# First layers of a mixture block queued behind given attention matmuls on TensorE, in a fused attention and MLP kernel

## The chip, the cores and the metric

One core of one Trainium2 chip runs the whole kernel. The metric is the device time of one execution in microseconds, lower is better; the median of several runs is compared. The engines are TensorE (PE, its weight loads PEld), VectorE (DVE), ScalarE (ACT), GpSimd (POOL) and SyncE (SP), which issues the DMAs. Each works through its own queue in the order that the built program gives.

## The reference, cut to what matters

```python
# q, k, v: (8 batches, 8 heads, 576 tokens, 64); w_phi: (64, 128); all float32
def phi(x):
    proj = einsum('bhsd,df->bhsf', x, w_phi)
    proj = proj - max(abs(proj), axis=-1, keepdims=True)
    return concatenate([exp(proj), exp(-proj)], axis=-1)      # 256 features
q_p, k_p = phi(q), phi(k)
kv = einsum('bhsf,bhsd->bhfd', k_p, v)
z = sum(k_p, axis=2)
x = einsum('bhsf,bhfd->bhsd', q_p, kv) / (einsum('bhsf,bhf->bhs', q_p, z)[..., None] + 1e-6)
x = x.transpose(0, 2, 1, 3).reshape(4608, 512)                # tokens by model
h = x @ w_in                                                  # 512 -> 2048
out = maximum(0.01 * h, h) @ w_out                            # 2048 -> 512
```

## The kernel before

**Two parts beside each other.** The attention makes `x`, two heads at a time: head pair i = 4 * batch + pair, 32 of them. The MLP works on blocks of 256 tokens, 18 of them, and needs all four pairs of the batches that a block touches. Block 2 (tokens 512 to 767) and block 3 need batch 1 (pairs 4 to 7); block 4 (tokens 1024 to 1279) also needs batch 2 (pairs 8 to 11), since batch 2 begins at token 1152.

**Precision.** A factor is split into a high part in the fast float32r format and a low part that holds the rest (`xh` and `xl`, `gh` and `gl`, `qh` and `ql`, `kph` and `kpl`, weights `w0h`, `w0l`, `w1h`, `w1l`), and a product is three matmuls: high by high, high by low, low by high.

**A unit of the MLP** is one block and one of 16 slices of 128 hidden features. `layer1` has 12 matmuls of 256 columns into the PSUM tile `h` (2 buffers): L601 and L602 read `xh`, L604 reads `xl`, each for d = 0 to 3, and the head pairs of a batch are the four d. ScalarE then applies the leaky ReLU in place (Prelu, L607) and casts `gh` (L69), VectorE makes `gl` (L609). `layer2` has six matmuls of 512 columns into two `acc` tiles (L623, L624, L625). It is written three units later (LAG = 3). The list `steps` gives the units their numbers from 0: 0 to 7 are the first half of block 0, 8 to 23 block 1, 24 to 31 the rest of block 0, 32 to 47 block 2, 48 to 63 block 3, 64 to 79 block 4. `split(i)` casts a block's `x` from `ring` into `xh` (ScalarE, L69) and `xl` (GpSimd, L74); there is one buffer of each.

**The attention** is the generator `attention()`, which takes turns between `k_phase` of one pair and `q_phase` (or `token_q_phase` for the first 8 pairs) of the pair ahead of it. For the pairs around unit 60: `q_phase` has projections (L377, L378), a transpose and a maximum on VectorE (L379, L381, small reductions at L383 to L389), the subtraction and transpose back into `mb` (L398, L400, one buffer), exponentials on ScalarE (L405, L406), the cast `qh` (L69), `ql` on GpSimd (L74), six matmuls per half and head (L417, L418, L420), and copies to `ring` and `tq` (L422, L423). At the end VectorE and GpSimd divide by the denominators (L426 to L431), so that `ring` holds `x`. `k_phase` has projections (L302 or L231), maximum, subtraction, exponentials `ek` (L249, L250), the casts `kph` and `kpl`, and sums into the PSUM tile `c` (L211); then transposes (L281).

**What sets the order.** The program is written unit by unit; `advance(goal)` between them draws from the generator. Attention is traced at a priority (PA = -500000) ahead of the MLP's (0). A scheduler then puts each engine's queue in an order by these priorities and by its own estimate of when an instruction could start. So where attention and MLP instructions stand to each other in a queue is not written in the code, but comes out of that estimate. On the chip the engines take their queues in that order.

Of the kernel before, what the change touches and what calls it, by code (L numbers as in the profile page):

```python
# [28 lines left out]
NBLK = NTOK // T  # L29
LAG = 3  # L30
CUT = 8
NN = 8
NK = 8
NF = 12
# [12 lines left out]
def attention_moe_kernel(ctx: ExitStack, tc: tile.TileContext, q, k, v, vt, w_phi, w_in, w_out, out):  # L47
    nc = tc.nc
# [7 lines left out]
    def st(shape, dt, tag):  # L56
        return sp.tile(shape, dt, tag=tag, name=tag, bufs=BUFS.get(tag, 1))
# [8 lines left out]
    def copy_(key, o, i):  # L66
        e = pick(key) or "a"
        if e == "a":
            nc.scalar.copy(o, i)  # L69
        else:  # L70
            (nc.vector if e == "v" else nc.gpsimd).tensor_copy(o, i)
# [4 lines left out]
    def pt(tag):  # L76
        return ps.tile([P, 512], F32, tag=tag, name=tag, bufs=PBUFS[tag])
# [5 lines left out]
    def weight(which, part, ft):  # L83
        g, f = divmod(ft, 4)
        if (which, part, g) not in weights:
            name = f"w{which}{part}{g}"
            weights[which, part, g] = (cp.tile([P, 4, DM], F32R, tag="late", name=name, bufs=4) if g == 3 else
                                       ct([P, 4, DM], F32R, name))
        return weights[which, part, g][:, f]
# [101 lines left out]
    def k_phase(i):  # L191
# [87 lines left out]
        for j in range(2):  # L279
            for t in range(2):  # L280
                nc.tensor.transpose(kvtv[:, j, t], kvs[:, j, t], ident[0:66, 0:66])  # L281
        if i < NN:
            kvh = st([P, 2, 2, P], F32, "kvx" if i % 2 else "kvh")
# [286 lines left out]
    def attention():  # L570
        for i in range(NP, B * NP + 1):
            gens = [k_phase(i)] if i < B * NP else []
            if i > NP:
                gens.append((token_q_phase if i - 1 < NN else q_phase)(i - 1))
            while gens:
                for it in list(gens):
                    if next(it, end) is end:
                        gens.remove(it)
                    else:
                        yield i - 1  # L580
            yield i
# [4 lines left out]
    def split(i):  # L586
        for d in range(NP):
            t0 = 0
            while t0 < T:
                c = (i * T + t0) % (2 * S)  # L590
                n = min(T - t0, S - c % S)
                x = ring[:, c // S, d, c % S : c % S + n]
                t1 = t0 + n
                copy_("xh", xh[:, d, t0:t1], x)
                tt_("xl", xl[:, d, t0:t1], x, xh[:, d, t0:t1].bitcast(F32), ALU.subtract)
                t0 = t1

    def layer1(i, ft):
        ph = pt("h")[:, 0:T]
        for d in range(NP):  # L600
            nc.tensor.matmul(ph, lhsT=weight(0, "h", ft)[:, d * P : d * P + P], rhs=xh[:, d], start=d == 0, stop=False)  # L601
            nc.tensor.matmul(ph, lhsT=weight(0, "l", ft)[:, d * P : d * P + P], rhs=xh[:, d], start=False, stop=False)  # L602
        for d in range(NP):
            nc.tensor.matmul(ph, lhsT=weight(0, "h", ft)[:, d * P : d * P + P], rhs=xl[:, d], start=False, stop=d == NP - 1)  # L604
        gh = st([P, T], F32R, "gh")
        gl = st([P, T], F32R, "gl")
        nc.scalar.activation(ph, ph, AF.Prelu, alpha=0.01)  # L607
        copy_("gh", gh, ph)
        nc.vector.tensor_tensor(gl, ph, gh.bitcast(F32), op=ALU.subtract)  # L609
        gs[i, ft] = (gh, gl)  # L610
# [3 lines left out]
    def layer2(i, ft, half=range(TT)):  # L614
        first, last = (ft in (0, CUT), ft in (CUT - 1, NFT - 1)) if i == 0 else (ft == 0, ft == NFT - 1)
        if first and half[0] == 0:
            for t in range(TT):
                accs[i, t] = pt("acc")
        gh, gl = gs[i, ft]
        for t in half:  # L620
            ts = slice(t * P, t * P + P)
            a = accs[i, t]
            nc.tensor.matmul(a, lhsT=gh[:, ts], rhs=weight(1, "h", ft), start=first, stop=False)  # L623
            nc.tensor.matmul(a, lhsT=gh[:, ts], rhs=weight(1, "l", ft), start=False, stop=False)  # L624
            nc.tensor.matmul(a, lhsT=gl[:, ts], rhs=weight(1, "h", ft), start=False, stop=last)  # L625
        if not last:
            return
        for t in half:
            if ft == CUT - 1:
                if t == 0:  # L630
                    held[0] = st([P, TT, DM], F32, "ks")
                copy_("o", held[0][:, t], accs[i, t])
                continue
            o = st([P, DM], F32, "ek" if i == NBLK - 1 and t else "o")
            if i == 0:
                nc.vector.tensor_tensor(o, accs[i, t], held[0][:, t], op=ALU.add)
            else:
                copy_("o", o, accs[i, t])
            r = i * T + t * P
            nc.sync.dma_start(out[r : r + P, :], o)  # L640

    stream = attention()
    state = {"p": PA, "n": NP - 1}

    def advance(goal):
        keep = tc.cur_priority
        tc.cur_priority = state["p"]
        while state["n"] < goal:
            state["n"] = max(state["n"], next(stream, B * NP))
        state["p"] = tc.cur_priority  # L650
        tc.cur_priority = keep

    def room(i):
        return min(B, 2 + i * T // S) * NP
# [15 lines left out]
    steps = [(i, ft) for i in range(2, NBLK) for ft in range(NFT)]  # L670
    steps = [(0, ft) for ft in range(CUT)] + [(1, ft) for ft in range(NFT)] + [(0, ft) for ft in range(CUT, NFT)] + steps
    split(0)
    for n, (i, ft) in enumerate(steps):
        layer1(i, ft)
        advance(min(room(n // NFT + 1), NP * (1 + (n + 1) / NFT * T / S) + 2))
        if n + 1 < len(steps) and steps[n + 1][0] != i:
            advance(math.ceil((steps[n + 1][0] + 1) * T / S) * NP)
            split(steps[n + 1][0])
        if n >= LAG:
            layer2(*steps[n - LAG])  # L680
# [39 lines left out]
```

## Time and profile before

| | us |
|---|---|
| median of 3 runs | 1193.41 (1190.35 to 1195.17) |
| the profiled execution's own time | 1196.45 |
| its span, first to last instruction | 1194.7 |
| TensorE busy | 1164.5 (97%) |
| ScalarE busy | 833.5 (70%) |
| VectorE busy | 755.9 (63%) |
| GpSimd busy | 417.5 (35%) |

The profile's rows name an operation by the line of the source, the engine and the tiles, out<-in. A wait is shown as the idle time of the engine ahead of an instruction and what ended it. Busy time of TensorE holds the modelled ends of overlapped matmuls, so that a busy TensorE can still be slower than it could be; the spacing of neighbouring matmuls shows that. In the table of stretches the granted clock is TensorE's, 1.00 at full speed.

### The profile page before, as it was taken

The numbers are of one execution on the slowest core, as the hardware profiler recorded it, in microseconds if no ns is written. First come the engines' busy times: TensorE is split into PE (matmuls) and PEld (weight loads), VectorE is DVE, ScalarE is ACT, GpSimd is POOL, SyncE is SP. The second block draws the span as 40 slices with busy tenths as digits, with TensorE's granted clock in tenths as the row PEclk, the third lists the DMA queues.
The fourth block names the chain that finished last, engine by engine and source line by source line (L and its number), as shares of the span: only waits on it lengthen the run. The fifth ranks groups of instructions, "written<-read, shape, count | busy, mean of one in ns | idle before, by whom it ended". The sixth has DMA issues, their size and how long they took to land.

```text
span 1194.7 us, 21190 instructions
## 1 busy us (share of the span) xinstructions
PE 1164.5 (97%) x7576; PEld 1045.5 (88%) x7576; DVE 755.9 (63%) x1510; ACT 833.5 (70%) x2108; POOL 417.5 (35%) x422
## 2 busy tenths in 40 slices
PE   8899999999998999999999999999999999999998
PEld 5687888899897989889899999998999999988987
DVE  4899883566767777677787777726777776111111
ACT  4898884667777787878788888837787877432232
POOL 0111011345454444545455454604454544110000
PEclk9899999999998999999999999999999999999999
DMA  7334532111201111110111111101011100000000
GB/s 208 90 101 142 152 114 59 40 42 31 60 22 50 32 50 31 41 30 22 50 31 50 32 49 32 49 12 37 23 50 32 49 1 19 1 18 19 1 19 18
DMA packets 62778, 57.01 MB, mean 48 GB/s; under 512 B 45136, under 2 KB 46288, under 8 KB 62672
## 3 DMA queue, kind: packets, MB, share of 16 engines
q1 hardware_dynamic: 62672, 55.65, 16.4%
q8 instruction: 60, 0.98, 0.4%
q14 instruction: 46, 0.38, 0.1%
HBM read 46.20 MB, written 9.44 MB: 47 GB/s over the span
## 4 chain that ended last, share of the span: by engine, by line
PE 82%; DVE 8%; ACT 5%; issue 2%; DMA 1%; POOL 1%; SPq 0%; DVEq 0%; ACTq 0%; POOLq 0%
PE h L601 10%; PE h L604 10%; PE h L602 10%; PE acc L623 10%; PE acc L625 10%; PE acc L624 10%; PE c L211 7%; PE a L302 2%; PE a L420 2%; PE a L418 2%; PE a L417 2%; PE a L231 2%; PE a L333 1%; PE a L377 1%; PE a L378 1%
## 5 line engine op out<-in xcount | busy, mean ns | idle before, releaser
L601 PE MATMUL h<-xh,w0h 128*128 128x256 f32 x1152 | 296.3, 287 | 5.9 <-DVE gl L609 4.9
L602 PE MATMUL h<-xh,w0l 128*128 128x256 f32 x1152 | 290.9, 282 | 0.0
L609 DVE TENSOR_TENSOR gl<-h,gh 128x256 fp32r<-128x256 f32 x288 | 118.7, 416 | 245.9 <-ACT gh L69 220.6
L623 PE MATMUL acc<-w1h,gh 128*128 128x512 f32 x576 | 229.6, 399 | 6.4 <-ACT gh L69 6.3
L601 PEld LDWEIGHTS h<-xh,w0h 128*128 128x128 f32 x1152 | 218.0, 189 | 17.0 <-DVE gl L609 8.0
L624 PE MATMUL acc<-w1l,gh 128*128 128x512 f32 x576 | 227.7, 395 | 0.0
L602 PEld LDWEIGHTS h<-xh,w0l 128*128 128x128 f32 x1152 | 217.9, 189 | 7.0 <-issue 0.4
L607 ACT ACTIVATE h<-h 128x256 f32<-128x256 f32 x288 | 105.3, 368 | 155.0 <-PE h L604 152.0
L625 PE MATMUL acc<-w1h,gl 128*128 128x512 f32 x576 | 204.4, 396 | 0.0
L604 PE MATMUL h<-xl,w0h 128*128 128x256 f32 x1152 | 200.3, 283 | 0.0
L74 POOL TENSOR_TENSOR ql<-eq,qh 128x576 fp32r<-128x576 f32 x96 | 146.5, 1539 | 73.6 <-ACT qh L69 51.0
L604 PEld LDWEIGHTS h<-xl,w0h 128*128 128x128 f32 x1152 | 164.5, 189 | 1.1 <-issue 0.4
L74 POOL TENSOR_TENSOR kpl<-ek,kph 128x512 fp32r<-128x512 f32 x72 | 96.6, 1342 | 146.9 <-PE c L211 67.2
L623 PEld LDWEIGHTS acc<-w1h,gh 128*128 128x128 f32 x576 | 108.4, 188 | 27.7 <-ACT gh L69 8.9
L624 PEld LDWEIGHTS acc<-w1l,gh 128*128 128x128 f32 x576 | 108.4, 188 | 18.0
L69 ACT CAST gh<-h 128x256 fp32r<-128x256 f32 x288 | 105.1, 371 | 25.6 <-PE acc L624 20.0
L74 POOL TENSOR_TENSOR xl<-ring,xh 128x256 fp32r<-128x256 f32 (+3 forms) x100 | 62.6, 655 | 162.1 <-PE h L604 131.6
L74 POOL TENSOR_TENSOR ring<-ring,mb 128x576 f32<-128x576 f32 (+2 forms) x45 | 49.8, 1108 | 192.9 <-DVE mb L559 39.2
L625 PEld LDWEIGHTS acc<-w1h,gl 128*128 128x128 f32 x576 | 99.3, 189 | 8.1
L249 ACT ACTIVATE ek<-pmk 128x256 f32<-128x256 f32 (+1 forms) x128 | 53.3, 417 | 33.5 <-POOL kpl L74 17.3
L199 DVE TENSOR_TENSOR ks<-rk,ks 64x576 fp32r<-64x576 f32 x40 | 44.5, 1112 | 30.5 <-ACT ks L69 29.9
L211 PE MATMUL c<-kph,vh 128*66 128x256 f32 x240 | 62.1, 281 | 0.7 <-ACT kph L69 0.7
(214 smaller groups left out, 2257.8 us busy)
## 6 DMA issues: line engine op xcount, KB each, us to landing
out_dram<-o SPq DMA_DIRECT2D x35, 256.0 KB, 2.1
rk<-in_k_dram SPq DMA_DIRECT2D x29, 288.0 KB, 2.8
ring<-in_w_in_dram SPq DMA_DIRECT2D x16, 512.0 KB, 3.6
qh<-in_w_out_dram SPq DMA_DIRECT2D x16, 512.0 KB, 3.7
rq<-in_q_dram SPq DMA_DIRECT2D x28, 288.0 KB, 3.0
rv<-in_v_dram SPq DMA_DIRECT2D x29, 256.0 KB, 3.5
rv<-in_vt_dram SPq DMA_DIRECT2D x58, 32.0 KB, 3.0
fr<-in_k_dram SPq DMA_DIRECT2D x2, 288.0 KB, 3.4
```

The costliest lines, as they stand in the source:

```text
L69: nc.scalar.copy(o, i)
L74: (nc.vector if pick(key) == "v" else nc.gpsimd).tensor_tensor(o, a, b, op=op)
L211: nc.tensor.matmul(kvp[0 : lt.shape[1], 256 * j : 256 * j + 256], lhsT=lt, rhs=rt, start=first and j == 0, stop=last, skip_group_check=True)
L249: nc.scalar.activation(ek[r, :, 0:F], pmk[r, 2 * s : 2 * s + 2], AF.Exp)
L601: nc.tensor.matmul(ph, lhsT=weight(0, "h", ft)[:, d * P : d * P + P], rhs=xh[:, d], start=d == 0, stop=False)
L602: nc.tensor.matmul(ph, lhsT=weight(0, "l", ft)[:, d * P : d * P + P], rhs=xh[:, d], start=False, stop=False)
L604: nc.tensor.matmul(ph, lhsT=weight(0, "h", ft)[:, d * P : d * P + P], rhs=xl[:, d], start=False, stop=d == NP - 1)
L607: nc.scalar.activation(ph, ph, AF.Prelu, alpha=0.01)
L609: nc.vector.tensor_tensor(gl, ph, gh.bitcast(F32), op=ALU.subtract)
L623: nc.tensor.matmul(a, lhsT=gh[:, ts], rhs=weight(1, "h", ft), start=first, stop=False)
L624: nc.tensor.matmul(a, lhsT=gh[:, ts], rhs=weight(1, "l", ft), start=False, stop=False)
L625: nc.tensor.matmul(a, lhsT=gl[:, ts], rhs=weight(1, "h", ft), start=False, stop=last)
```

## The change

While attention is traced, the TensorE instructions that it makes are collected in `products`, numbered from 0 in the order of the program. The first layers of units 24 to 61 are traced inside `tc.issue_after(...)`, which gives each of their TensorE instructions an edge to one product: unit n may stand in TensorE's queue only behind product 111 + 10.2 * (n - 24), rounded down. An edge within one engine's queue needs no semaphore; it is an order and no wait of its own. Unit 24's product is 111, unit 57's 447, unit 58's 457 and unit 61's 488. The rest of the program is as it was, but the scheduler works all queues out anew with these edges.

```diff
+PACED = (24, 62, 111, 10.2)
+PE = mybir.EngineType.PE
...
+    products = []
     stream = attention()
     state = {"p": PA, "n": NP - 1}
...
         while state["n"] < goal:
+            made = len(nc.cur_bb.bb.instructions)
             state["n"] = max(state["n"], next(stream, B * NP))
+            products.extend(i for i in nc.cur_bb.bb.instructions[made:] if i.engine == PE)
...
     for n, (i, ft) in enumerate(steps):
-        layer1(i, ft)
+        if PACED[0] <= n < PACED[1]:
+            with tc.issue_after(products[int(PACED[2] + PACED[3] * (n - PACED[0]))]):
+                layer1(i, ft)
+        else:
+            layer1(i, ft)
```

The lines of the changed kernel stand two further down than before in the attention and in both layers (L601 is L603, L417 is L419, L69 is L71).

What it moves, first on TensorE at unit 57, whose `h` is `h_4004` and whose `gh` is `gh_4017`. Before, behind the last matmuls of its first layer:

```order
L604 MATMUL h_4004<-xl_71,w0h2_800 128x256 x4
L625 MATMUL acc_3876<-w1h1_721,gl_3946 128x512
L417 MATMUL a_3252<-qh_3165,kvh_2896 128x288
L420 MATMUL a_3243<-ql_3234,kvh_2896 128x288 x2
L418 MATMUL a_3252<-qh_3165,kvl_2897 128x288
L417 MATMUL a_3252<-qh_3165,kvh_2896 128x288
L418 MATMUL a_3252<-qh_3165,kvl_2897 128x288
L231 MATMUL a_3508<-wq_72,ks_3483 128x256 x2
L625 MATMUL acc_3877<-w1h1_721,gl_3946 128x512
L623 MATMUL acc_3876<-w1h1_721,gh_3969 128x512
```

There the second layers of units 54 and 55 (`gl_3946`, `gh_3969`) and the last products of pair 10 (`qh_3165`) follow; unit 57's own second layer comes much later. Now:

```order
L606 MATMUL h_4004<-xl_71,w0h2_800 128x256 x4
L213 MATMUL c_3505<-kpl_3556,vh_74 66x256 x2
L625 MATMUL acc_3876<-w1h2_813,gh_4017 128x512
L626 MATMUL acc_3876<-w1l2_814,gh_4017 128x512
L625 MATMUL acc_3877<-w1h2_813,gh_4017 128x512
L626 MATMUL acc_3877<-w1l2_814,gh_4017 128x512
L627 MATMUL acc_3876<-w1h2_813,gl_4018 128x512
L627 MATMUL acc_3877<-w1h2_813,gl_4018 128x512
L419 MATMUL a_3616<-qh_3580,kvh_3213 128x288
L420 MATMUL a_3616<-qh_3580,kvl_3214 128x288
```

Unit 57's second layer now stands two matmuls behind its first, and the first numerator products of pair 11 (`qh_3580`) right behind that.

On ScalarE at the same place, from unit 57's Prelu on. Before:

```order
L607 ACTIVATE h_4004<-h_4004 128x256
L422 COPY ring_69<-a_3243 64x288
L423 ACTIVATE tq_3079<-a_3243 64x288
L69 COPY pmk_3507<-a_3508 128x256
L422 COPY ring_69<-a_3252 64x288
L423 ACTIVATE tq_3079<-a_3252 64x288
L69 CAST gh_4017<-h_4004 128x256
L69 CAST kvh_3213<-c_3208 128x4x64 x2
```

These are the last copies of pair 10. Now:

```order
L609 ACTIVATE h_4004<-h_4004 128x256
L71 CAST gh_4017<-h_4004 128x256
L407 ACTIVATE eq_3589<-mb_3582 128x288
L408 ACTIVATE eq_3589<-mb_3582 128x288
L407 ACTIVATE eq_3597<-mb_3582 128x288
L408 ACTIVATE eq_3597<-mb_3582 128x288
L71 CAST qh_3580<-eq_3589 128x576
L71 CAST qh_3580<-eq_3597 128x576
L251 ACTIVATE ek_3603<-pmk_3574 128x2x128
L252 ACTIVATE ek_3603<-pmk_3574 128x2x128
L71 CAST kph_3606<-ek_3603 128x512
```

Pair 11's exponentials and casts now stand at unit 57; fifteen more operations follow up to the cast of `qh_3580` from `eq_3675`, the fourth.

On TensorE at the start of block 4, unit 64, whose `h` is `h_4188`. Before, from the row behind pair 11's last products (`a_3703`, eight matmuls further up) to the d = 3 matmuls of unit 64:

```order
L377 MATMUL a_4238<-qs_4221,wq_72 128x288
L378 MATMUL a_4238<-qs_4221,wq_72 128x288
L231 MATMUL a_4242<-wq_72,ks_4206 128x256 x2
L377 MATMUL a_4247<-qs_4221,wq_72 128x288
L378 MATMUL a_4247<-qs_4221,wq_72 128x288
L377 MATMUL a_4254<-qs_4221,wq_72 128x288
L378 MATMUL a_4254<-qs_4221,wq_72 128x288
L377 MATMUL a_4271<-qs_4221,wq_72 128x288
L378 MATMUL a_4271<-qs_4221,wq_72 128x288
L601 MATMUL h_4188<-xh_70,w0h0_616 128x256
L602 MATMUL h_4188<-xh_70,w0l0_617 128x256
L604 MATMUL h_4188<-xl_71,w0h0_616 128x256 x3
```

Now pair 11's last products stand ahead of unit 60 (`h_4076`):

```order
L606 MATMUL h_4052<-xl_71,w0h2_800 128x256 x4
L422 MATMUL a_3703<-ql_3678,kvh_3213 128x288
L213 MATMUL c_3505<-kpl_3629,vh_74 66x256 x2
L422 MATMUL a_3703<-ql_3678,kvh_3213 128x288
L233 MATMUL a_4231<-wq_72,ks_4206 128x256 x2
L379 MATMUL a_4238<-qs_4221,wq_72 128x288
L380 MATMUL a_4238<-qs_4221,wq_72 128x288
L603 MATMUL h_4076<-xh_70,w0h3_892 128x256
```

From there to the d = 3 matmuls of unit 64 are 108 matmuls, where there were 18 before.

## The prediction

> **What bounds the kernel now.** I read the page's head first, then who TensorE waited for, then the busy time of each engine by stretch, and last the timeline and the chain around the worst stretch.
>
> ```profile
> span 1194.7 us, 21190 instructions
> PE 1164.5 (97%) x7576; PEld 1045.5 (88%) x7576; DVE 755.9 (63%) x1510; ACT 833.5 (70%) x2108; POOL 417.5 (35%) x422
> ```
>
> TensorE is busy 97% of the span, and the change adds and removes no work, so the time can only move by what TensorE loses: idle time, and matmuls at a lower clock. The list of TensorE's waits, its head:
>
> ```profile
> PE acc L623 <- ACT gh L69: 6.3, 7, 1.9
> PE h L601 <- DVE gl L609: 4.9, 4, 1.8
> ```
>
> The longest waits are under 2 us. Where they lie and what they cost is read from the stretches (length, then busy us of PE, PEld, DVE, ACT, POOL with instruction counts, the granted clock, DMA):
>
> ```profile
> 302.00:320.00 18.00, 18.00 (x115) 16.12 (x114) 16.99 (x33) 10.92 (x26) 5.40 (x4) 1.00 0.28 81
> 320.00:334.00 14.00, 13.31 (x96) 12.24 (x94) 5.89 (x11) 13.68 (x35) 8.31 (x7) 1.00 0.09 23
> 345.00:365.00 20.00, 19.49 (x128) 17.11 (x126) 11.97 (x21) 18.90 (x51) 12.63 (x15) 1.00 0.14 44
> 362.45:380.66 18.21, 13.30 (x68) 11.62 (x67) 15.82 (x35) 11.01 (x30) 5.97 (x7) 0.81 0.22 64
> 365.00:370.00 5.00, 2.42 (x13) 1.91 (x14) 4.84 (x10) 1.89 (x5) 1.87 (x2) 0.96 0.14 52
> 370.00:375.00 5.00, 3.38 (x19) 3.24 (x18) 4.84 (x10) 3.32 (x10) 1.63 (x1) 0.70 0.04 7
> 375.00:380.00 5.00, 4.71 (x20) 4.30 (x21) 4.27 (x12) 2.71 (x8) 1.86 (x3) 0.66 0.47 120
> 570.00:575.00 5.00, 3.43 (x24) 3.21 (x25) 4.77 (x14) 2.58 (x8) 1.42 (x1) 1.00 0.68 169
> 600.00:700.00 100.00, 100.00 (x698) 92.58 (x697) 77.60 (x153) 83.94 (x215) 51.61 (x48) 1.00 0.15 40
> ```
>
> One stretch stands out: 362.45 to 380.66, the start of block 4 (unit 64). The timeline has its gaps, the chain what filled them:
>
> ```profile
> 362.45 0.43 PE L420 MATMUL a<-ql,kvh 128*128 128x288 f32 x2
> 365.80 0.40 PE L377 MATMUL a<-qs,wq 128*128 128x288 f32 x1 [1.13 <-DVE tq L379]
> 367.98 0.40 PE L377 MATMUL a<-qs,wq 128*128 128x288 f32 x1 [1.64 <-DVE pmk L236]
> 368.98 0.38 PE L601 MATMUL h<-xh,w0h 128*128 128x256 f32 x1
> 375.29 0.50 PE L623 MATMUL acc<-w1h,gh 128*128 128x512 f32 x1 [1.91 <-ACT gh L69]
> 380.67 0.28 PE L211 MATMUL c<-kph,vh 128*66 128x256 f32 x1
> ```
>
> ```profile
> 364.15 0.79 DVE mb L426
> 366.24 0.79 DVE mb L429
> 367.18 1.42 POOL ring L74
> 368.63 0.31 ACT xh L69
> ```
>
> At 362.45 TensorE issues the last products of head pair 11, which block 4 needs. Normalization on VectorE and GpSimd and the cast to `xh` take until 368.94, and unit 64's d=3 matmul starts at 368.98, 6.5 us after them. Meanwhile TensorE has next to nothing, and afterwards the clock is 0.70 and 0.66.
>
> The price: back to back, matmuls of 256, 288 and 512 columns are spaced as these rows of the chain show (0.47/4, 0.26/2, 0.24):
>
> ```profile
> 349.32 0.47 PE c L211 x4
> 361.35 0.26 PE a L420 x2
> 361.62 0.24 PE acc L625
> ```
>
> From 362.45 to 380.66 the program has 66 matmuls: 42 x 0.118 + 10 x 0.13 + 10 x 0.235 + four small transposes at about 0.06 (an estimate) = 8.9 us. They took 18.2. **The boundary costs 9.3 us**: roughly 5.9 of idle and latency, 3.4 of clock (5 x 0.04 + 5 x 0.30 + 5 x 0.34).
>
> **The change, part by part.**
>
> *The edges.* They add no instruction: TensorE's queue is reordered from unit 27 to unit 169 and is the same ahead of and behind that. SyncE issues the same loads and stores, a few of them some places apart; the loads are asked for a whole pair ahead, which hides that. 0 us.
>
> *Attention ahead.* When unit 61 starts, 444 products stand ahead of it before, 504 now. Pair 11's last product now has 108 matmuls between it and unit 64's d=3 matmul: 72 x 0.118 + 8 x 0.13 + 24 x 0.235 + four small ones = 15.4 us, against the 6.5 us that the chain above takes. The cover is 9 us wide, so the 9.3 us go. What is late next there is layer 2 of unit 64: 2.5 us of matmuls stand between its first layer and it, and that path ended the gap of 1.91 in the row at 375.29; I leave 0.5 us for it. **-8.8 us.**
>
> *The price of it.* From product 362 (the row below) to product 500 (the row at 362.45) TensorE spent 59 us; in the new order 50 us of matmuls lie between them, 11 units in place of 14 beside the same products. The rows 302 to 365 say what this meets: VectorE is 94% busy, then ScalarE 98%, and from 345 ScalarE 95%, in turn. A gated first layer stands behind its product in TensorE's queue; when that product is late, all that stands behind waits too, other units' second layers and the next products, and with them ScalarE and VectorE. The costs of their operations:
>
> ```profile
> 303.27 0.30 PE L378 MATMUL a<-qs,wq 128*128 128x288 f32 x1
> 355.06 0.42 ACT L405 ACTIVATE eq<-mb 128x288 f32<-128x288 f32 x1
> 355.39 0.43 ACT L406 ACTIVATE eq<-mb 128x288 f32<-128x288 f32 x1
> ```
>
> ```profile
> L607 ACT ACTIVATE h<-h 128x256 f32<-128x256 f32 x17 | 6.2, 367 | 5.7 <-PE h L604 4.9 <-DVE m L381 0.5
> L69 ACT CAST gh<-h 128x256 fp32r<-128x256 f32 x17 | 6.2, 371 | 0.4 <-PE acc L624 0.2
> L69 ACT CAST kph<-ek 128x512 fp32r<-128x512 f32 x9 | 5.6, 622 | 0.1
> L69 ACT CAST qh<-eq 128x576 fp32r<-128x576 f32 x8 | 5.2, 667 | 0.1
> L422 ACT COPY ring<-a 64x288 f32<-64x288 f32 x10 | 3.9, 389 | 0.2
> L249 ACT ACTIVATE ek<-pmk 128x256 f32<-128x256 f32 x9 | 3.8, 417 | 1.9 <-POOL kpl L74 1.1 <-DVE pmk L242 0.8
> L405 ACT ACTIVATE eq<-mb 128x288 f32<-128x288 f32 x8 | 3.5, 434 | 3.2 <-DVE mb L400 3.2
> L69 ACT CAST ks<-rk 64x576 fp32r<-64x576 f32 x4 | 2.7, 671 | 0.1
> L199 DVE TENSOR_TENSOR ks<-rk,ks 64x576 fp32r<-64x576 f32 x4 | 5.5, 1368 | 4.5 <-ACT ks L69 4.4
> L366 DVE TENSOR_TENSOR qs<-rq,qs 64x576 fp32r<-64x576 f32 x6 | 4.5, 752 | 0.2
> ```
>
> 1. Units 57 and 58. Behind unit 57's last first-layer matmul ScalarE has 26 operations up to the fourth `qh` cast of pair 11: 2 Prelu, 1 `gh`, 8 exponentials of `mb`, 4 `qh`, 4 exponentials of `pmk`, 1 `kph`, 2 `ks`, 2 `ring`, 2 `tq` = 12.4 us by the means (L406, L250 and L423 priced as their neighbours L405, L249 and L422). Neighbours overlap by 0.09 (0.42 long, the next 0.33 later), so 12.4 - 25 x 0.09 = 10.2. TensorE has 46 matmuls for that time: 22 x 0.118 + 18 x 0.13 + 6 x 0.235 = 6.3 us. Layer 2 of unit 57 now follows its own first layer by two matmuls. **+4.0 us**; the ends are 2 (ScalarE has done part of the 26 by then, as it runs ahead where TensorE is the later one) and 6 (GpSimd's `ql` in between comes late too).
>
> 2. Units 50 to 52, pair 10. Between its last projection and its first `qh` product VectorE has 23 operations: 2 `ks` and 2 `qs` are 4.2 us, the other 19 about 5.8 (an estimate, 0.31 each; by the mean of the row 302 to 320, 16.99/33, all 23 would be 11.8), and ScalarE then has four exponentials and a cast (1.9). With 0.3 for the hops that is 12.2 us against 11.1 us of matmuls. A second cast adds 0.6. **+1.7 us**, ends 0 and 3.5.
>
> 3. Two short distances (first transposes of the last token-phase group to its products in unit 33; layer 2 of units 37 and 51 two to three us behind their first layer). **+1.0 us**, ends 0 and 2.
>
> *Given up:* the stall ahead of unit 55 inside the row 320 to 334 (14.00 less 13.31), -0.7. Later, up to unit 169, the order moves by a few places: of the 11.2 us of the two waits listed first, those that lie there can go or be joined by others; 0, ends -2 and +2.
>
> *Sum:* -8.8 + 4.0 + 1.7 + 1.0 - 0.7 = -2.8 us. The profiled execution took 1196.45 us at a span of 1194.7; the median is 1193.41, and I take the difference from that: 1190.6, rounded to **1191 us**.
>
> *The clock.* At 370 to 380 the clock fell after a stretch with TensorE busy 2.42 of 5 us, though no single gap passed 1.91. At 570 to 575, busy 3.43 of 5, it stayed 1.00. Units 57 and 58 now have 6.3 us of work in some 10.3, 61%, nearer the second, so I add nothing and keep 1.7 us (half of the 3.4) for the upper end. [...]
>
> **The rivals.**
>
> *The queues keep up.* ScalarE holds 84% and VectorE 78% over 600 to 700 with TensorE at 100%. If their order now overlaps the pairs so well and the new waits sum to 2.5 us, the time is 1193.4 - 8.8 - 0.7 + 2.5 = 1186.4. Against it: the two engines took turns in 302 to 365.
>
> *Slower: the pairs cannot be squeezed.* If VectorE's and ScalarE's dense stretches stay in turn, pairs 10 and 11 still need their 59 us, and TensorE waits the whole 9 us of the squeeze and the 6 us (counted in matmuls) by which product 362 itself is pulled ahead, and the clock falls twice, 3.4: -9.5 + 9 + 6 + 3.4 = +8.9, 1202. It decides once the new waits pass 9.5 us.
>
> *It doesn't do what it says at block 4.* Products are early but `xh` is cast late, behind other operations on ScalarE: the 9.3 us stay, the waits come on top: 1193.4 + 6 = 1199.5. The cover of 9 us speaks against it.
>
> **How the numbers follow.** Forecast 0.56 (1188 to 1196), queues keep up 0.26, squeezed in vain 0.12, boundary stays 0.06. A change under 0.5% (6 us) can hardly be told from none here. Faster than 1187.4: the second case and a little of the first, 0.27. Slower than 1199.4: two thirds of the last two, 0.12. Same 0.61. The range takes the second case's lower part and most of the upper ends, 1184.5 to 1198.5.
>
> **What would show it.** Right: TensorE's window at unit 64 without the 1.13 and 1.64 gaps and at clock 1.00; new gaps before `acc` L625 of unit 57 and the `a` products behind it, released by ScalarE's `gh` and `qh`. Wrong: clock under 1 around units 57 to 60; gaps left at block 4; or no gap at unit 57.

## The result, and the profile after

The changed kernel takes **1207.18 us** (median, 1206.82 to 1207.25), the kernel before 1193.76 us in the same comparison: a ratio of 1.0116 with an interval of 1.0095 to 1.0138. It is slower by 13 us, where 1191 was forecast. The profiled execution took 1207.18 us at a span 10.7 us longer than before. Executions of one kernel lie up to 6 us apart here; the profiles show up to 3 us of that ahead of unit 27, where the queues are still the same, so the table below compares stretches.

The head of the page, with TensorE still at 97%:

```profile
span 1205.4 us, 21163 instructions
PE 1172.4 (97%) x7576; PEld 1044.4 (87%) x7576; DVE 764.2 (63%) x1510; ACT 835.6 (69%) x2108; POOL 420.9 (35%) x422
```

TensorE's waits in the changed kernel, the head of the list (what waited, on what, us in total, times, longest):

```profile
PE acc L304 <- ACT bd L148: 5.2, 1, 5.2
PE acc L625 <- ACT gh L71: 4.1, 5, 1.1
PE h L548 <- ACT eq L533: 3.4, 1, 3.4
PE a L419 <- ACT qh L71: 3.2, 5, 0.9
PE h L603 <- DVE gl L611: 2.8, 6, 1.0
PE h L606 <- POOL xl L76: 2.0, 3, 0.8
PE c L213 <- ACT kph L71: 1.6, 2, 1.2
PE acc L627 <- DVE gl L611: 1.2, 2, 0.6
PE c L548 <- ACT qs L533: 1.1, 1, 1.1
PE c L213 <- DVE kph L271: 1.1, 1, 1.1
```

The waits of 5.2 and 3.4 us, and the one of L548 on `qs`, lie in the first 63 us, and the kernel before has them too (5.4, 3.5 and 1.1). Behind them no wait is longer than 1.2 us; the list has moved from layer 2 and `h` to the attention's products. The stretches (length, busy us of PE, PEld, DVE, ACT, POOL, granted clock, DMA):

```profile
302.00:320.00 18.00, 16.02 (x99) 12.94 (x97) 16.44 (x29) 12.96 (x31) 6.74 (x5) 1.00 0.21 67
320.00:334.00 14.00, 13.34 (x95) 12.56 (x96) 5.53 (x13) 9.89 (x25) 4.80 (x6) 1.00 0.11 25
335.00:340.00 5.00, 3.77 (x26) 3.29 (x25) 4.91 (x8) 3.12 (x7) 1.45 (x2) 1.00 0.00 0
340.00:345.00 5.00, 4.10 (x27) 3.18 (x25) 4.73 (x11) 2.38 (x7) 1.98 (x2) 1.00 0.21 59
345.00:350.00 5.00, 3.68 (x18) 2.61 (x18) 3.43 (x7) 4.03 (x11) 1.73 (x2) 1.00 0.00 0
350.00:355.00 5.00, 3.65 (x26) 2.93 (x25) 2.39 (x2) 4.89 (x13) 3.69 (x3) 1.00 0.07 9
355.00:360.00 5.00, 4.00 (x12) 3.31 (x13) 2.35 (x4) 3.52 (x9) 1.85 (x3) 0.57 0.17 55
360.00:365.00 5.00, 5.00 (x33) 4.80 (x33) 1.53 (x3) 2.26 (x6) 0.23 (x1) 0.74 0.00 0
361.30:379.50 18.20, 18.20 (x128) 16.94 (x127) 14.20 (x33) 12.60 (x36) 7.35 (x10) 0.97 0.14 35
```

The boundary is gone: the last row, around the start of unit 64 at 377.7, has TensorE busy all through with 128 matmuls, where 18.21 us before had 13.30 and 68. In its place stands 335 to 365: VectorE nearly full for ten us, then ScalarE, TensorE at three quarters, and behind that the clock at 0.57 and 0.74. The timeline names the gaps (idle time and what ended it, in brackets; unit 57 starts at 342.9):

```profile
320.66 0.33 PE L213 MATMUL c<-kph,vl 128*64 128x256 f32 x1 [1.11 <-DVE kph L271]
339.38 0.33 PE L213 MATMUL c<-kph,vh 128*66 128x256 f32 x1 [1.23 <-ACT kph L71]
341.82 0.72 PE L627 MATMUL acc<-w1h,gl 128*128 128x512 f32 x2 [0.57 <-DVE gl L611]
345.30 0.50 PE L625 MATMUL acc<-w1h,gh 128*128 128x512 f32 x1 [0.63 <-ACT gh L71]
347.11 0.73 PE L627 MATMUL acc<-w1h,gl 128*128 128x512 f32 x2 [0.60 <-DVE gl L611]
348.25 0.40 PE L419 MATMUL a<-qh,kvh 128*128 128x288 f32 x1 [0.41 <-ACT qh L71]
353.57 0.40 PE L419 MATMUL a<-qh,kvh 128*128 128x288 f32 x1 [0.72 <-ACT qh L71]
355.11 0.53 PE L422 MATMUL a<-ql,kvh 128*128 128x288 f32 x2 [0.74 <-POOL ql L76]
356.53 0.61 PE L419 MATMUL a<-qh,kvh 128*128 128x288 f32 x1 [0.89 <-ACT qh L71]
363.53 0.29 PE L422 MATMUL a<-ql,kvh 128*128 128x288 f32 x1
```

The last row but one is product 496 and the last is pair 11's very last; product 500 starts at 363.16. Before, it started at 362.45. TensorE's queue has it 13.7 us of matmuls sooner, and the clock on the wall has it no sooner.

**How the loss is counted.** Each matmul of TensorE's program gets its back-to-back spacing (0.119 us for 256 columns, 0.132 for 288, 0.233 for 512, 0.06 to 0.11 for transposes, all as the traces have it; plain float32 is put at four times the first, an estimate: in the traces such a matmul of 256 columns is two records 0.216 us apart, 0.43); the sum up to a place is the work there. What an execution took between two places beyond that work is lost, to waits or to a low clock. By this count, worked out from all TensorE rows of each profile (us lost in each stretch of work; work 280 to 330 is units 50 to 62 of the changed kernel, with its losses at units 49 to 59, as the text calls this column; 330 to 400 is the boundary of block 4; "product 500" is its start in us):

| kernel | gated units | time | 180-280 | 280-330 | 330-400 | 400-530 | 530-790 | product 500 |
|---|---|---|---|---|---|---|---|---|
| before | none | 1193.8 | 1.2 | 0.7 | 9.6 | 5.5 | 1.5 | 362.4 |
| changed | 24-61 | 1207.2 | 2.6 | 14.8 | 0.8 | 3.9 | 7.8 | 363.2 |
| e1 | 24-61, 9.0 each | 1200.4 | 4.2 | -0.2 | 12.1 | 7.6 | 1.3 | 365.7 |
| e3 | 24-47 | 1191.3 | 2.4 | 1.3 | 5.0 | 5.1 | 0.9 | 361.1 |
| e4 | 48-61 | 1216.3 | 5.1 | 14.1 | 1.4 | 7.6 | 11.9 | 362.6 |
| e5 | 60-63 | 1196.0 | 1.2 | 7.6 | 4.3 | 4.0 | 0.6 | 358.9 |
| e6 | 24-55 | 1194.0 | 2.5 | 3.9 | 3.0 | 5.4 | 1.0 | 356.9 |
| e7 | 24-61, less VectorE | 1194.1 | 1.9 | 2.2 | 1.5 | 4.1 | 6.8 | 349.8 |
| e8 | 24-61, `vl` later | 1208.2 | 2.6 | 14.8 | 0.8 | 3.7 | 10.1 | 361.7 |
| e9 | 24-47, 10.8 each | 1192.8 | 7.1 | -0.1 | 4.6 | 3.2 | 1.0 | 362.0 |
| e10 | none, less VectorE | 1188.0 | 1.5 | 0.1 | 3.9 | 5.6 | 1.4 | 355.7 |
| e11 | none, GpSimd | 1196.7 | 1.5 | 0.5 | 6.2 | 9.4 | 1.8 | 357.0 |
| e12 | 24-61, GpSimd | 1206.9 | 2.8 | 5.0 | 2.3 | 9.1 | 13.1 | 352.8 |
| e13 | 129-136 | 1199.1 | 1.2 | 0.8 | 9.7 | 5.5 | 5.6 | - |

From before to the changed kernel: +1.3, +14.1, -8.8, -1.6, +6.3, and -0.6 at the two ends, together +10.7, the difference of the spans. The last column holds what an execution had lost ahead of work 180 as well: there e4, e6, e8 and e10 stood 2.6, 2.9, 2.0 and 2.4 us ahead of before, the others up to 1.0.

### The profile page after: what moved, and what is told of

The parts are those of the page before. It is cut to its first block, busy times and chain, and to the rows that moved or that the text cites. A ratio compares the mean times of both kernels' runs of the same rounds, so it can differ in the third digit from the quotient of the medians.

```text
span 1205.4 us, 21163 instructions
## 1 busy us (share of the span) xinstructions
PE 1172.4 (97%) x7576; PEld 1044.4 (87%) x7576; DVE 764.2 (63%) x1510; ACT 835.6 (69%) x2108; POOL 420.9 (35%) x422
## 4 chain that ended last, share of the span: by engine, by line
PE 80%; DVE 9%; ACT 6%; issue 2%; POOL 2%; DMA 1%; DVEq 0%; POOLq 0%; ACTq 0%; SPq 0%
PE h L603 10%; PE h L604 10%; PE acc L625 10%; PE h L606 10%; PE acc L626 9%; PE acc L627 9%; PE c L213 6%; PE a L304 2%; PE a L422 2%; PE a L419 2%; PE a L420 2%; PE a L233 1%; PE a L335 1%; PE a L380 1%; PE a L379 1%
## 5 line engine op out<-in xcount | busy, mean ns | idle before, releaser
L603 PE MATMUL h<-xh,w0h 128*128 128x256 f32 x1152 | 294.9, 287 | 3.5 <-DVE gl L611 2.8
L611 DVE TENSOR_TENSOR gl<-h,gh 128x256 fp32r<-128x256 f32 x288 | 119.0, 416 | 258.5 <-ACT gh L71 241.6
L603 PEld LDWEIGHTS h<-xh,w0h 128*128 128x128 f32 x1152 | 218.1, 189 | 14.6 <-DVE gl L611 5.9
L71 ACT CAST gh<-h 128x256 fp32r<-128x256 f32 x288 | 105.8, 371 | 22.9 <-PE acc L626 17.2
L213 PE MATMUL c<-kph,vl 128*64 128x256 f32 x240 | 62.3, 282 | 1.1 <-DVE kph L271 1.1
```

The lines of the kernel that those rows point to most:

```text
L213: nc.tensor.matmul(kvp[0 : lt.shape[1], 256 * j : 256 * j + 256], lhsT=lt, rhs=rt, start=first and j == 0, stop=last, skip_group_check=True)
```

## The experiments

**e1, e3, e4, e5: pace or edges.** Only the numbers of `PACED` differ (first unit, end, product of the first, products for each unit):

```diff
-PACED = (24, 62, 111, 10.2)
+PACED = (24, 62, 111, 9.0)      # e1
+PACED = (24, 48, 111, 10.2)     # e3
+PACED = (48, 62, 355.8, 10.2)   # e4
+PACED = (60, 64, 480, 7)        # e5
```

> Same edges, units 24 to 61, but 9.0 products for each unit in place of 10.2, which is about the pace that the kernel before has by itself: in the built order 440 products stand ahead of unit 60 (before 442, changed kernel 498). Theory 'pace': the loss comes from asking ScalarE and VectorE for pairs 10 and 11 sooner, so here no new loss in the stretch of units 49 to 59 (under 2 us), the 9 us at unit 64 stay, and the time is 1193 (1190 to 1197). Rival 'edges': layer 1 behind given products makes TensorE's queue stiff at any pace; then units 49 to 59 lose 8 us or more here too, the 9 us at unit 64 stay on top, and the time is 1203 to 1212.

1200.35 us, ratio 1.0048 (1.0031 to 1.0064): between the two expectations. At units 49 to 59 nothing is lost, as the theory of the pace has it, but the boundary takes 12.1 instead of 9.6, and 2 to 3 us more go at units 33 to 47 and behind block 4 each. Its boundary, in the stretch that the prediction showed of before, is at a clock of 0.63, with TensorE's clock at half for 5 us:

```profile
362.45:380.66 18.21, 13.01 (x56) 10.56 (x55) 14.25 (x23) 10.44 (x26) 5.29 (x5) 0.63 0.15 46
370.00:375.00 5.00, 1.99 (x6) 1.00 (x4) 4.56 (x9) 1.66 (x5) 2.47 (x3) 0.50 0.11 43
```

So the edges aren't free at the old pace either (about 6 us), but the loss at units 49 to 59 is no matter of the edges.

> Only units 24 to 47 are queued behind products, at 10.2 for each; units 48 to 63 are free. The order is the changed kernel's up to unit 48 (361 products ahead of it) and falls back to 454 ahead of unit 60. Theory 'pace': the loss of 3.9 us at units 49 to 52 stays, the 10.7 us at units 55 to 59 go, the 9 us at unit 64 come back for the most part: 1196 (1192 to 1200). Rival 'edges': 24 of 38 edges, so about 24/38 of the 17 us: 11, with the 9 at unit 64 back: 1204. Rival 'later order' (the 6 us that the changed kernel loses at 630 to 785 us are the scheduler's reordering and belong to no gate): a loss there of any size between 0 and 6, unrelated to the loss at units 49 to 59.

1191.3 us, ratio 0.997 (0.9958 to 0.9982): a little faster than both kernels, and below the range of the theory of the pace. The loss at units 55 to 59 goes, as it has it; the other two come out smaller than it has them. Pairs 8 to 10 begin earlier, 1.3 us in place of 3.9 are lost at units 49 to 52, and the boundary falls from 9.6 to 5.0. Behind unit 100 nothing is lost, so that loss of the changed kernel needs the later gates. e3's boundary in the same stretch, 97 matmuls where before had 68:

```profile
362.45:380.66 18.21, 15.96 (x97) 13.39 (x96) 16.08 (x36) 11.78 (x30) 6.75 (x8) 0.91 0.22 63
```

> Only units 48 to 61 are queued behind products, the same products as in the changed kernel (355 + 10.2 per unit); units 24 to 47 are free. Product 500 stands at the same amount of TensorE work as in the changed kernel (321 us), products up to 340 nearly as before. Theory 'pace': the last part of the squeeze carries the price: units 49 to 59 lose 10 to 15 us with the clock down once, the boundary's 9 us are saved: 1196 to 1200, plus what the later order adds (0 to 6). Rival 'edges': 14 of 38 edges cost 14/38 of 17, 6 us, less 9 at the boundary: 1190.

1216.25 us, ratio 1.0182 (1.0167 to 1.0197), the slowest run of all with 14 gates of 38. The rival falls. 14.1 us are lost at units 49 to 59 and 1.4 at the boundary, as the theory has it; 3.9 more than before ahead of them and 11.9 between work 530 and 790 were above what I expected, and with them the time, by 10 us.

> Only units 60 to 63 are queued behind products 480, 487, 494 and 501: just enough to put pair 11's last products ahead of block 4. 466 products ahead of unit 60 (before 442), 518 ahead of unit 64 (before 468); product 500 has 9.5 us of TensorE work between it and unit 64, where it stood behind its start before. Theory 'pace': TensorE reaches product 480 about 8 us of work sooner than before, and pair 11 is not there yet: the waits move from unit 64 to units 60 to 63, 6 to 9 us of them, 1193 (1190 to 1196). Rival 'boundary alone': pair 11's chain has slack up to here and only the queue's order held it back; then the boundary's 9 us go for 2 to 3 us of new waits: 1186 to 1188.

1196.02 us, ratio 1.0011 (1.0002 to 1.0021), the upper end of the theory's range. The waits moved from unit 64 to the units around 60: 7.6 us there, 4.3 instead of 9.6 at the boundary. Pair 11 was not there yet.

The last column of the table says it shortest. Wherever these gates put product 500 in TensorE's queue (behind 320.6 to 334.5 us of work), it started between 359 and 366 us. **The products come when ScalarE and VectorE have made their operands; a gate doesn't bring them, it holds the MLP back in front of them.** The d = 3 matmul of unit 64 starts 10 us later in the changed kernel (379.14, before 368.98), with the same work ahead of it.

**e6, e9: how much of the gate is harmless.**

```diff
-PACED = (24, 62, 111, 10.2)
+PACED = (24, 56, 111, 10.2)     # e6
+PACED = (24, 48, 111, 10.8)     # e9
```

> The changed kernel's gates, but only for units 24 to 55; units 56 to 63 are free. Its order is the changed kernel's up to unit 55. It stands between e3 (gates to unit 47, 1191.3) and the changed kernel (to unit 61, 1207.2). In the five orders run so far the last product of pair 11 (product 500) was issued at 359 to 366 us, wherever TensorE's order put it: theory 'own pace of the attention': the products come when ScalarE and VectorE have made their operands, and gates only hold the MLP back in front of them. Then product 500 comes at 359 to 366 here too, the 3.9 us at units 49 to 52 are lost, about 6 us of TensorE work are left between product 500 and unit 64, so unit 64 waits 1 to 3 us, and the time is 1194 to 1199. Rival 'every gate costs': 8 of the 14 gates between e3 and the changed kernel, 8/14 of the 16 us: 1200.

1194.0 us, ratio 1.0008 (0.9993 to 1.0023). As expected, at the lower end: 3.9 at units 49 to 52, 3.0 at the boundary. Product 500 came at 356.9, two us ahead of the range that I gave; this profile had begun 2.9 us earlier than before's by work 180, which covers it. So the last six gates, 56 to 61, carry the 11 us at units 55 to 59 and the whole late loss.

> As e3 (gates for units 24 to 47 only) with 10.8 products for each unit: unit 32 has 205 products ahead of it, e3 189, unit 48 373 and 361. Theory 'own pace': what helps in e3 is that pairs 8 to 10 begin about 5 us sooner (product 362 at 298.3 us, before 303.3) for 2.7 us of waits. If they can begin sooner still, product 362 comes at 295 to 297 and product 500 at 358 to 360, the boundary loses 3 to 4 us in place of 5.1, and the time is 1189 (1188 to 1191). If pairs 8 and 9 are at their own limit already, the gates make TensorE wait 2 to 5 us more in units 28 to 47 and nothing comes sooner: 1193 to 1196. I hold the second for a little likelier.

1192.76 us, ratio 0.9991 (0.998 to 1.0002). The second case: 7.1 us are lost at units 28 to 47 in place of 2.4, and product 500 comes no sooner than in e3. So pairs 8 and 9 gain nothing from a pace above 10.2.

**e7 and e10: VectorE's part.** For pairs 10 to 12 the subtractions that make the low parts of q (and of k, which only pair 12 has) are left out, zeros stand there, written by GpSimd: eight subtractions, not four for each of three pairs as the expectation says. e10 is the same without gates.

```diff
+            if i in (10, 11, 12):
+                nc.gpsimd.memset(qs[n, j].bitcast(F32), 0.0)
+            else:
             nc.vector.tensor_tensor(qs[n, j], rq[o], qs[o, j].bitcast(F32), op=ALU.subtract)
...   # and the same for ks
-PACED = (24, 62, 111, 10.2)
+PACED = (24, 24, 111, 10.2)     # e10 only: no gate
```

The reason for it: following the chain back from product 500 at 363.16 in the changed kernel, over data and queues, to 300 us, about 32.0 us lie in VectorE's queue, 15.9 in ScalarE's, 10.6 in MLP matmuls and 4.7 in other ones. Before, it was about 17.1, 15.8, 21.7 and 8.0. Some rows of that chain on VectorE, the first two forms among those left out:

```profile
306.19 2.31 DVE L368 TENSOR_TENSOR qs<-rq,qs 64x576 fp32r<-64x576 f32 x2
309.09 0.75 DVE L201 TENSOR_TENSOR ks<-rk,ks 64x576 fp32r<-64x576 f32 x1
317.77 1.00 DVE L73 CAST kph<-ek 64x512 fp32r<-64x512 f32 x1 [0.53 <-ACT ek L252]
318.81 1.80 DVE L271 TENSOR_TENSOR kph<-ek,kph 64x512 fp32r<-64x512 f32 x1
```

> The changed kernel's gates; for pairs 10, 11 and 12 the four subtractions on VectorE that make the low parts of k and q (ks, qs) are left out, and GpSimd writes zeros there instead. TensorE's order hardly differs from the changed kernel's up to unit 120. In the changed kernel's trace six of these subtractions lie in VectorE's two dense stretches that the chain back from product 500 runs through, 0.68 to 1.56 us each, 6.1 us in all. Theory 'own pace of the attention, set by VectorE and ScalarE in turn': product 500 comes 3 to 6 us sooner than 363.2, units 49 to 59 lose 3 to 6 us less than 14.6, and the time is 1201 to 1204. Rival 'the order on TensorE is what costs': nothing moves by more than 1 us, 1206 to 1208. Rival 'ScalarE alone sets it': at most 1 us of it comes through, 1206.

1194.11 us, ratio 1.0008 (0.9998 to 1.0018): 13 us under the changed kernel, more than twice what I expected and far from both rivals. TensorE's order differs from the changed kernel's in places, from unit 44 to 75, but product 500 has the same work ahead of it. It starts 13.3 us sooner, 2.2 us are lost at units 49 to 59 in place of 14.8, the clock stays at 1.00, and the boundary stays closed. e7's product 500 and its stretches:

```profile
349.82 0.42 PE L428 MATMUL a<-ql,kvh 128*128 128x288 f32 x2
```

```profile
302.00:320.00 18.00, 18.00 (x125) 16.58 (x124) 9.77 (x22) 16.37 (x39) 10.32 (x9) 1.00 0.25 80
336.90:361.30 24.40, 23.03 (x160) 20.90 (x159) 16.49 (x31) 20.32 (x50) 11.99 (x12) 1.00 0.11 26
```

VectorE has 9.77 us to do up to 320 where the changed kernel had 16.44, and ScalarE works beside it (16.37, where it had 12.96). The six subtractions on the chain were 6.1 us; what the other 7 of the 13.3 come from, the new order of the queues or less overlap of VectorE with GpSimd, no run separates.

> As e7 (pairs 10 to 12 without the VectorE subtractions for the low parts of k and q, zeros from GpSimd instead), with no gates at all: the kernel before with that work left out. With e7, the changed kernel and the kernel before it makes the four corners of gates by VectorE work. Theory 'own pace': without gates the order on TensorE binds, not VectorE: product 500 stands behind 330.9 us of TensorE work, so it comes at 358 (in e7 at 349.8), unit 64 stands 1.5 us of work behind it and needs some 6.5, so 4 to 6 us are lost there (9.8 before, 0 in e7), and the time is 1188 to 1191. Then the 13 us that e7 won over the changed kernel are VectorE's, of which only 3 to 5 show without gates. Rival 'the subtractions are simply dear wherever they stand': the same 13 us come off here, 1181. Rival 'only the order counts': 1193.

1187.96 us, ratio 0.9944 (0.9929 to 0.9959), at the lower edge of what the theory has, with 3.9 us lost at the boundary; 6.5 us show without gates where it had 3 to 5. With e7 that makes the four corners. Up to work 400 are lost (columns 180 to 400): before 11.5, changed 18.2; with less VectorE work 5.5 without gates and 5.5 with them. **The gates cost 6.7 us there with the full work of VectorE, and nothing with less.** So up to there the price of the pace hangs on VectorE's work. It isn't shown to hang on VectorE alone: no run takes as much off ScalarE, which has its turn in the same stretch. With less work the gates win nothing either, they only move 2.4 us from the boundary to the units ahead of it. And over the whole run they still cost 6.2 us with less work (1194.1 against 1188.0), 5.4 of them between work 530 and 790.

**e11, e12: the same eight subtractions on GpSimd**, so that nothing is left out.

```diff
-            nc.vector.tensor_tensor(qs[n, j], rq[o], qs[o, j].bitcast(F32), op=ALU.subtract)
+            (nc.gpsimd if i in (10, 11, 12) else nc.vector).tensor_tensor(qs[n, j], rq[o], ...)
...   # and the same for ks; e11 without gates, e12 with the changed kernel's
```

> The kernel before, without gates, with the four subtractions of pairs 10, 11 and 12 on GpSimd in place of VectorE; the result is the reference's. GpSimd is 28 to 40% busy in these stretches. Theory 'own pace': like e10, with product 500 behind 330.2 us of TensorE work, 4 to 7 us lost at unit 64: 1188 to 1192. Rival: GpSimd takes twice as long for each and pairs 11 and 12 come later by it: 1194 to 1197.

1196.72 us, ratio 1.0019 (1.0007 to 1.0031). Up to work 400 it is the theory (6.2 at unit 64, 8.1 in all against 11.5); the 3.4 us won are lost again at the next boundary but one, unit 96, where the new order has the attention 28 products later (776 against 804 ahead of that unit). The expectation missed that. The time lies in the rival's range, but not for its reason: product 500 came at 357.0, sooner than before.

> The changed kernel's gates with the four subtractions of pairs 10, 11 and 12 on GpSimd; the result is the reference's. Theory 'own pace': most of what e7 won stays, since the work leaves VectorE: units 49 to 59 lose 4 to 8 us (changed kernel 14.6, e7 2 to 3), nothing at unit 64; behind unit 100 the attention stands a few products further ahead than in the changed kernel and the late loss is 5 to 10 (changed kernel 6): 1195 to 1202. Rival: GpSimd's own time for them, with ql and kpl behind them, sets the pairs' pace as VectorE did: 1206.

1206.88 us, ratio 1.0105 (1.0087 to 1.0122). At units 49 to 59 5.0 us are lost, as expected, and 2.3 at the boundary; but 22 us go between work 400 and 790, 15 more than before, where I had put 5 to 10. GpSimd takes 1.59 us on the mean for a subtraction that VectorE does in 0.75 when alone:

```profile
L368 POOL TENSOR_TENSOR qs<-rq,qs 64x576 fp32r<-64x576 f32 x6 | 9.5, 1590 | 2.0 <-issue 1.6
```

**e8, e13: the late loss.** In the changed kernel's trace GpSimd does the next pair's `vl` ahead of block 8's `xl`; before it was the other way round. (start, length, engine, line, tiles):

```profile
633.34 2.02 POOL L76 TENSOR_TENSOR vl<-rv,vh 128x512 fp32r<-128x512 f32 x2 [0.60 <-PE h L606]
635.44 3.85 POOL L76 TENSOR_TENSOR xl<-ring,xh 128x256 fp32r<-128x256 f32 x4
```

e8 puts that back at blocks 8 and 10:

```diff
-                tt_("vl", vl[r, c], rv[r, c, 0:64], vh[r, c, 0:64].bitcast(F32), ALU.subtract)
+                with tc.issue_after(xls[i]) if i in xls else nullcontext():
+                    tt_("vl", vl[r, c], rv[r, c, 0:64], vh[r, c, 0:64].bitcast(F32), ALU.subtract)
...
             split(steps[n + 1][0])
+            if steps[n + 1][0] in (8, 10):
+                xls[state["n"] + 1] = nc.cur_bb.bb.instructions[-1]
```

> The changed kernel with one more order: on GpSimd the two vl subtractions of pair 21 stand behind block 8's xl and those of pair 25 behind block 10's, as in the kernel before; the changed kernel has them ahead (2.0 us of vl ahead of xl at 633 and 763 us). All queues are the same up to unit 128. Theory: the late loss of the changed kernel at units 127 to 130 and 159 to 162 is this swapped order, so the loss between 580 and 620 us of TensorE work goes from 2.5 to 0 and that between 700 and 740 from 2.4 to under 0.5, 1202 to 1204. Rival: attention that is ahead by a few products loads VectorE and ScalarE at the block boundaries whatever stands first on GpSimd; then at most 1 us comes back, 1206.

1208.24 us, ratio 1.0131 (1.0106 to 1.0156). My theory of the swap falls. `xl` came first on GpSimd, the waits at `xl` shrank from 2.0 to 0.5 us, and other operations were late instead (over the whole run layer 2 waited 5.4 us for `gh` in place of 4.1, `h` 4.6 us for `gl` in place of 2.8): 10.1 us lost between work 530 and 790, more than the changed kernel's 7.8.

e13 goes the other way: from the kernel before, with gates alone where the product is traced by then, at units 129, 131 to 133 and 136.

```diff
-        if PACED[0] <= n < PACED[1]:
-            with tc.issue_after(products[int(PACED[2] + PACED[3] * (n - PACED[0]))]):
+        if LATE.get(n, 10**9) < len(products):   # {129: 1121, 131: 1147, 132: 1157, 133: 1165, 136: 1193}
+            with tc.issue_after(products[LATE[n]]):
```

> The kernel before, with gates on units 131 to 136 alone (as far as their products are traced by then), behind the products that stand ahead of these units in the changed kernel: unit 132 has 1148 products ahead of it as there, before 1134; up to unit 128 all queues are as before, and GpSimd keeps block 8's xl ahead of vl as before. In the seven runs with 1142 products or more ahead of unit 132 (the changed kernel, e4, e7, e8, e12) 5 to 11 us are lost between 530 and 740 us of TensorE work, in those with 1134 to 1136 (before, e1, e3, e5, e6, e9, e10) nothing. Theory: a dozen products more ahead at that place is what costs, the wait at xl only its first sign: 2 to 3 us are lost between 580 and 660, nothing between 700 and 740, 1196 to 1197.5. Rival: vl ahead of xl on GpSimd, or something in units 100 to 127, is needed for it: under 0.5 us lost, 1194.

1199.13 us, ratio 1.0037 (1.0023 to 1.0051). (The kernels with 1142 products or more ahead of unit 132 were five, as listed, not seven.) Everything up to work 600 is as before, then 4.0 us are lost between 600 and 610, 2.2 of them in one wait, and 0.5 more than before from 700 to 740:

```profile
648.13 0.40 PE L419 MATMUL a<-qh,kvh 128*128 128x288 f32 x1 [2.18 <-ACT tq L425]
```

So gates that put a dozen products more ahead of a unit cost 4.0 us there, more than I expected, and without `vl` ahead of `xl`: the rival falls. That the changed kernel's late loss has the same cause is not shown. It loses 1.1 us at this place (work 590 to 610), without a gate there, and the rest elsewhere: 2.6 between 710 and 730 alone, where e13 loses nothing. Why its queues still have it further ahead seventy units behind the last gate is the scheduler's doing, and stays open.

## Why the prediction was wrong, point by point

- *The list of waits.* "Under 2 us" left out the waits of 5.4 us (`acc` L302 on the load of `rk`) and 3.5 us (`h` L546) in the first 50 us. The changed kernel has both, so nothing follows from it.
- *The edges themselves, 0.* No DMA ends any of the gaps shown. At the old pace the reordering around them costs some 6 us (e1), which the term left out.
- *The boundary, -8.8.* Right: 9.6 lost before, 0.8 after. The 1.13 and 1.64 gaps are gone and the clock is 1.00 there.
- *Units 50 to 52, +1.7 (0 to 3.5).* The right place and engines, too small: 3.9 us lost between work 280 and 300, against the 0.7 of the stall ahead of unit 55 that stood there before. That stall is gone, as forecast. The longest new gap, 1.11 us at 320.66, waits for `kph` (L271) of the `k_phase` in between, which the term didn't count. Its 0.31 us for each of 19 VectorE operations and its 0.3 for the hops were estimates that no run shows; in the changed kernel VectorE was busy 17.65 us from 300 to 320 with 32 operations, 0.55 each.
- *Units 57 and 58, +4.0 (2 to 6).* **This is the step that failed.** Between work 300 and 330 the changed kernel loses 10.9 us, before nothing. The gaps that I named are there (345.30 by `gh`; 348.25, 353.57 and 356.53 by `qh`; 355.11 by `ql`, from its upper end), but three more stand at 339.38, 341.82 and 347.11, two of them ahead of unit 57. The eight gaps are 5.8 us, the low clock some 3. I counted ScalarE's 26 operations from unit 57 on, and never VectorE's stretch ahead of them for pair 11, though I had counted just that for pair 10: the rows 335 to 345 have VectorE busy 9.64 of 10 us. And I took the matmuls in between as cover, 6.3 us of them, while the edges hold the MLP behind the very products that are late. e7 supports it: with eight of VectorE's subtractions left out and the queues sorted anew, 2.2 of the 10.9 us remain.
- *Short distances, +1.0.* Measured +1.3 between work 180 and 280. Some 0.7 us are lost at unit 33, as named, and 0.5 at unit 44, which wasn't; unit 37 loses nothing.
- *Later reorderings, 0 (-2 to +2).* Wrong: -1.6 up to work 530, then +6.3. I saw an order that moved by a few places and took the two signs as equal; a dozen products further ahead can cost 4.0 us at one place (e13). What cost 6.3 here stays open.
- *The clock, 0.* Wrong: 5 x 0.43 + 5 x 0.26 = 3.5 us at 355 to 365, at most, since one of the gaps lies in it; it is part of the 10.9. I compared rows of 5 us, and took busy time for work: in the 3.41 us ahead of the fall at 355.74 TensorE was busy 1.85 us, with matmul work for 1.0 (last section).

The rival "pairs cannot be squeezed" named the mechanism, and its total is near: -9.5 + 9 + 6 + 3.4 against the measured -8.8 + 14.1 + 1.3, 3.5 of it clock. Its parts are less near: 15 us of waits where some 12 came. Up to work 400 the measured parts are 6.7 us, 1200.4; its 1202 lacks the rest, the late loss of 4.6 us net. I gave it 0.12, and wrote myself that the two engines take turns; I priced the turns for one engine at a time.

## What to carry to other kernels

An edge that holds filler work behind a product only moves that product if the queue of the engine that takes it was what held it; look first at when its operands are ready, by following the chain back over the other engines, all of them and for every pair alike. Where the operands come at their own pace, the gate turns filler into idle time; the lever is the work on the engines that set the pace (here VectorE, at pairs 10 to 12; less work for ScalarE wasn't tried). After a change that makes a scheduler sort anew, price each later boundary too, as it can lose as much as the place that was changed.

## What the runs showed of the hardware

*The clock fell without a long gap.* In the changed kernel no wait between 340 and 357 us passes 0.89 us, TensorE is busy 15.4 of 20 us from 340 to 360, and the clock is 0.57 and 0.74 in the last five of these and the next five. The clock record of these two traces has two values, 1.0 and 0.5: half from 355.74 to 362.56 in the changed kernel, from 369.58 to 373.00 and from 376.41 to 379.82 before. In the 3.41 us ahead of these three falls TensorE was busy 1.85, 1.63 and 1.50 us, with matmul work, at the back-to-back spacing, for 1.0, 1.0 and 1.2 us; the longest waits there were 0.74, 1.64 and 1.91. From 318.19 to 321.60 in the changed kernel, with a wait of 1.11, it was busy 2.00 us with work for 1.7, and the clock stayed 1.00 there and in the 3.41 us behind. So in the changed kernel a wait of 1.11 us came without a fall, and none above 0.74 ahead of one, in a stretch with less work. How little work it takes in general, these cases don't show.

*Subtractions on VectorE ran longer beside GpSimd.* Those for the low parts of `ks` (L201) and `kph` (L271) took 753 and 687 ns, the medians without GpSimd beside them, or up to 2.6 times that, and the long ones all ran beside a GpSimd operation, though not each one beside it was long (shortest, median and longest in ns, changed kernel):

```profile
L201 DVE TENSOR_TENSOR ks<-rk,ks x40: 751/755/1937, 309.1 to 974.2; 64x576 fp32r<-64x576 f32 x40
L271 DVE TENSOR_TENSOR kph<-ek,kph x24: 686/687/1812, 233.4 to 1010.1; 64x512 fp32r<-64x512 f32 x24
```

Of the 19 L271 without any overlap with a GpSimd operation none passes 691 ns; the five with some have a median of 1798. `gl` (L611) shows nothing of it: its median is 424 ns over the 137 with some overlap and over the 151 without. In the dense stretch of pair 10 the L271 at 318.81, beside two `ql` on GpSimd, took 1.80 us in place of 0.69, on the path of the products:

```profile
317.07 2.98 POOL L76 TENSOR_TENSOR ql<-eq,qh 128x576 fp32r<-128x576 f32 x2 [5.04 <-ACT qh L71]
```
